# Idle matmuls, earlier casts, all score pairs ahead of the sums and a halved down-projection in batch 0 of a Linformer-attention and maxout-FFN kernel

## The chip, the cores and the metric

The kernel runs on one NeuronCore of a Trainium2 chip. The metric is the device time of one execution in microseconds (us). Span means the profiled stretch of an execution; in most of these runs it is about 1.8 to 2.1 us shorter than the time. The profile lists for every run its span and the mean granted TensorE clock, and I use the spans where a few tenths matter. All runs used here were of the state "fast". Ratios are the mean time of one kernel's fast runs over that of the other's of the same rounds, so they are not quite the ratio of the medians that I quote.

PE is TensorE, PEld its weight loads, DVE is VectorE, ACT is ScalarE, POOL is GpSimd, SP is SyncE. L203 is line 203 of that kernel's source; line numbers differ between kernels. An idle matmul is one on a zero tile whose result nobody reads. A landing is the moment when a DMA's data has arrived. "jt" counts the six slices of 128 into which the 768 hidden columns are cut. "The batch-1 projection" is the first matmul of L116, the k projection of batch 1; I use its start as the end of the tail of batch 0.

## The reference

```python
# q, k, v: (8 batches, 8 heads, 1024, 64); E, F: (64, 1024); x: (8192, 512)
k_proj = einsum('ks,bhsd->bhkd', E, k)
v_proj = einsum('ks,bhsd->bhkd', F, v)
attn   = softmax(q @ k_proj^T / 8)            # over 64 projected keys
x      = (attn @ v_proj), heads joined        # (8192, 512)
h      = max(x @ w1, x @ w2, x @ w3)          # w: (512, 768)
out    = h @ w_out                            # w_out: (768, 512)
```

## The kernel before

Eight batches run in a software pipeline: while PE does the feed-forward part of batch b, the attention of batch b+1 is woven in. Batch 0 has nothing to hide behind, so it has a hand-written head: E and F are turned, q is cast and turned, k and v are projected as their DMAs land, and the first w1 slices follow. A batch is worked in two halves of 512 tokens; half 1 of batch 0 has its sums and value products woven into the down-projection of half 0.

```python
def warmup(n, bank):                       # idle matmuls on a zero tile
    for _ in range(n):
        nc.tensor.matmul(out=ps[:, bank, :], lhsT=warm[:, 0:P], rhs=warm, start=True, stop=True)

warmup(9, 7)                               # at the very start
... cast E, F; turn them on PE; evacuate eT on VectorE, fT on ScalarE ...
q_cast0(0)                                 # even head on ScalarE, odd head on VectorE
q_cast0(1)
q_turn0(0)                                 # four 128x128 transposes, then a VectorE copy
q_cast0(2)
q_turn0(1)
k_proj0(0)                                 # 16 small matmuls, then a VectorE copy
q_cast0(3)
q_turn0(2)
k_proj0(1)
q_turn0(3)
scores0(0, 0, SB[0]); exp0(0, 0, SB[0])
for g in range(2, NPAIR):                  # NPAIR = 4
    k_proj0(g)
    scores0(0, g - 1, SB[g - 1]); exp0(0, g - 1, SB[g - 1])
    warmup(1, 3)
sums_part0(0)                              # sums of heads 0..3: PE, then 1/sum as Exp(-Ln(sum)) on ScalarE
scores0(0, 3, SB[3]); exp0(0, 3, SB[3])
warmup(1, 3)
...
v_proj0(0, 3)
sums_part0(1)
warmup(1, 2)
v_proj0(1, 3)
av0(0, 0); av0(1, 0)                       # value products, heads 0..3
norm0(0, 0, 6, (0,)); norm0(0, 1, 7, (0,)) # VectorE: product * 1/sum -> xT
v_proj0(2, 3)
warmup(1, 2)
w1_ct(0)                                   # first w1 slice, 6 matmuls
v_proj0(3, 7)
w1_ct(1, range(3))                         # second w1 slice
av0(0, 1); av0(1, 1)
norm0(0, 0, 5, (1,)); norm0(0, 1, 6, (1,))
w1_ct(1, range(3, NJT)); w1_ct(2); w1_ct(3)
...
# the feed-forward of batch 0, half 0; "slot" counts ticks, and attention pieces start at a slot
groups = [(10, q_up0), (11, scores_up0), (13, lambda: sums0(1, 4)), (15, av_up0), (19, g1[0]), ...]
# the up-projections of half 0 use up slots 1 to 12, then
for tt in range(4):
    down(0, 0, 0, tt)                      # six matmuls over jt, evacuated by ScalarE
    tick()                                 # slot 13: sums of half 1; slot 15: its value products
```

After the four `down` calls PE takes the first up-projection of half 1 (L179 in both kernels), which reads what the four normalisations of half 1 write.

The softmax here doesn't subtract the row's maximum and nothing guards it: scores larger than these inputs give would overflow.

## Time and profile before

| what | before |
|---|---|
| time, median of the first 3 runs | 401.39 us (401.13 to 401.98) |
| profiled run | 402.01 us, span 400.0 us |
| PE wait for the first q cast | 0.99 us |
| second w1 slice starts | 22.00 us |
| first down matmul to the batch-1 projection | 39.84 to 49.38 us, 9.54 us |

The page of the kernel before: the first line is busy time, share of the span and instructions of each engine; the three digit lines cut the span into 40 slices of 10 us and give busy tenths, tenths of the granted TensorE clock, and busy tenths of the DMA engines; the last is the chain of work that ended last.

```profile
PE 393.4 (98%) x2420; PEld 170.0 (43%) x2420; DVE 185.7 (46%) x268; ACT 166.3 (42%) x250; POOL 70.8 (18%) x109
...
PE   7999999999999999999999999999999999999996
...
PEclk9699999999999999999999999999999999999999
DMA  9999969999932995149970899129981111102023
...
PE 94%; DMA 2%; DVE 1%; issue 1%; ACT 1%; POOL 0%; POOLq 0%; DVEq 0%
```

PE bounds the kernel, and after 50 us nothing but PE's own matmuls does. Only the first slices hold something to gain: PE is at 7 in the first, its clock is at 6 in the second, and DMA runs at 9 through them all.

Two stretches of the windows view of the kernel before (length of the stretch; busy us of PE, PEld, DVE, ACT and POOL, each with its instructions; granted clock, DMA share, GB/s):

```profile
9.00:13.00 4.00, 3.72 (x61) 2.27 (x61) 2.24 (x9) 0.78 (x2) 1.91 (x4) 0.59 1.24 205
13.00:17.00 4.00, 4.00 (x43) 1.38 (x43) 0.23 (x1) 2.38 (x5) 1.48 (x3) 0.55 1.22 205
```

The clock stands at half for most of 9 to 17 us. The trace's clock record puts the half stretch at 9.75 to 16.58 us.

PE's part of the timeline of the kernel before (start, us, what it does, and in brackets how long PE was idle before it and what ended that):

```profile
8.24 0.70 PE L340 MATMUL ps<-ident,q_t 128*128 128x128 bf16 x8 [0.99 <-ACT q_t L345]
...
14.58 0.61 PE L296 MATMUL ps<-warm 128*128 128x512 bf16 x1
...
22.00 0.82 PE L376 MATMUL ps<-xT,w_sb 128*128 128x512 bf16 x3
...
39.84 1.46 PE L203 MATMUL ps<-wo_sb,hT 128*128 128x512 bf16 x6
41.23 0.41 PE L218 MATMUL ps<-pT,ones 64*32 64x512 bf16 x8
41.57 2.76 PE L203 MATMUL ps<-wo_sb,hT 128*128 128x512 bf16 x12
44.27 0.62 PE L218 MATMUL ps<-pT,vp 64*32 64x512 bf16 x16
...
46.75 2.70 PE L179 MATMUL ps<-xT,w_sb 128*128 128x512 bf16 x11 [0.24 <-DVE xT L257]
...
49.38 0.40 PE L116 MATMUL ps<-k_t,eT 128*64 128x512 bf16 x1
```

In the tail of batch 0, PE does six down matmuls, the sums (41.23), twelve more, the value products (44.27), the last six, and then waits a little for VectorE. ScalarE and VectorE of the same stretch:

```profile
42.88 1.06 ACT L247 ACTIVATE rinv<-lns 128x1024 f32<-128x1024 f32 x1
...
44.81 2.48 DVE L257 TENSOR_TENSOR xT<-ps,rinv 128x512 bf16<-128x512 f32 x4 [4.07 <-PE ps L218]
```

The reciprocal is ready at 43.94 us, and the four normalisations start at 44.81 on the value products (L218), not on the reciprocal.

### The profile page before, as it was taken

The page shows a single profiled execution, that of the slowest core. Times are in us where ns is not written, and L with a number is a line of the kernel's source. Part 1 is how long each engine was busy: PE and PEld are TensorE (multiplying, and loading weights), DVE is VectorE, ACT ScalarE, POOL GpSimd, SP SyncE. Part 2 cuts the span into 40 slices and gives each one's busy share as a digit, 9 for nine tenths or more (in the row PEclk, how much of TensorE's full clock was granted, in tenths as well). Part 3 has the DMA queues.
Part 4 walks back from the last instruction along what each step waited for, and adds up shares of the span by engine and source line. Part 5 has one row for each costly group of instructions (what it writes and reads, how often), then busy time and mean ns, then how long its engine had stood idle before and what let it go on. Part 6 is the DMA issues. An engine that isn't in the chain of part 4 may idle for free.

```text
span 400.0 us, 5988 instructions
## 1 busy us (share of the span) xinstructions
PE 393.4 (98%) x2420; PEld 170.0 (43%) x2420; DVE 185.7 (46%) x268; ACT 166.3 (42%) x250; POOL 70.8 (18%) x109
## 2 busy tenths in 40 slices
PE   7999999999999999999999999999999999999996
PEld 4444353444444444444444444444444444444443
DVE  3246454554744365533744256443655337433441
ACT  3413557346324553247222652245532472222222
POOL 7351141150002401060000600024010000000000
PEclk9699999999999999999999999999999999999999
DMA  9999969999932995149970899129981111102023
GB/s 220 206 209 206 207 159 197 212 163 201 163 99 66 174 181 173 62 99 172 217 151 13 159 190 231 53 66 168 201 158 60 61 52 53 54 0 107 1 104 107
DMA packets 62651, 53.73 MB, mean 134 GB/s; under 512 B 30496, under 2 KB 57632, under 8 KB 62624
## 3 DMA queue, kind: packets, MB, share of 16 engines
q0 software_dynamic: 31760, 43.52, 53.9%
q1 hardware_dynamic: 30032, 8.92, 15.7%
q10 hardware_dynamic: 832, 0.92, 0.7%
q8 instruction: 19, 0.31, 0.3%
q14 instruction: 8, 0.07, 0.0%
HBM read 57.15 MB, written 16.78 MB: 185 GB/s over the span
## 4 chain that ended last, share of the span: by engine, by line
PE 94%; DMA 2%; DVE 1%; issue 1%; ACT 1%; POOL 0%; POOLq 0%; DVEq 0%
PE ps L179 59%; PE ps L203 20%; PE ps L116 3%; PE ps L145 3%; PE ps L383 3%; PE ps L135 2%; DMA k_t<-in_k_dram 2%; PE ps L376 1%; PE ps L218 1%; DVE xT L160 1%; PE ps L238 1%; DVE xT L257 0%; PE ps L288 0%; PE ps L224 0%; PE ps L296 0%
## 5 line engine op out<-in xcount | busy, mean ns | idle before, releaser
L179 PE MATMUL ps<-xT,w_sb 128*128 128x512 bf16 x1080 | 246.6, 379 | 0.2 <-DVE xT L257 0.2
L179 PEld LDWEIGHTS <-w_sb 128*128 128x128 bf16 x1080 | 103.2, 98 | 132.7 <-issue 12.8
L184 DVE TENSOR_TENSOR m<-ps,h1s 128x512 f32<-128x512 f32 x90 | 62.2, 691 | 143.0 <-PE ps L179 114.8
L203 PE MATMUL ps<-wo_sb,hT 128*128 128x512 bf16 x378 | 91.2, 379 | 0.0
L182 ACT COPY h1s<-ps 128x512 f32<-128x512 f32 x90 | 52.7, 586 | 65.5 <-PE ps L179 65.2
L205 ACT COPY o_acc<-ps 128x512 f32<-128x512 f32 x63 | 36.9, 586 | 99.9 <-PE ps L203 99.9
L210 POOL DMA_DIRECT2D out_dram<-o_acc x30 | 21.2, 706 | 285.4 <-ACT o_acc L205 285.4
L186 DVE TENSOR_TENSOR hT<-ps,m 128x512 bf16<-128x512 f32 x90 | 62.3, 692 | 13.7 <-PE ps L179 5.2
L203 PEld LDWEIGHTS <-hT 128*128 128x128 bf16 x378 | 35.7, 98 | 47.2 <-issue 6.0
L160 DVE TENSOR_TENSOR xT<-ps,rinv 128x1024 bf16<-128x1024 f32 x28 | 32.9, 1217 | 7.8 <-PE ps L145 7.8
L138 ACT ACTIVATE pT<-ps 128x1024 bf16<-128x1024 f32 x28 | 27.1, 1021 | 13.4 <-PE ps L135 13.4
L87 POOL DMA_DIRECT2D v_t<-in_v_dram x21 | 15.3, 760 | 3.3 <-PE ps L376 1.7
L152 ACT ACTIVATE lns<-ps 128x1024 f32<-128x1024 f32 x14 | 13.6, 1021 | 1.9 <-PE ps L145 1.9
L155 ACT ACTIVATE rinv<-lns 128x1024 f32<-128x1024 f32 x14 | 14.2, 1062 | 0.0
L116 PE MATMUL ps<-k_t,eT 128*64 128x512 bf16 x56 | 13.4, 382 | 0.0
L118 PE MATMUL ps<-v_t,fT 128*64 128x512 bf16 x56 | 13.4, 382 | 0.0
L87 POOL DMA_DIRECT2D q_t<-in_q_dram x14 | 10.7, 771 | 4.3 <-DMA q_t<-in_q_dram 1.9
L383 PE MATMUL ps<-xT,w_sb 128*128 128x512 bf16 x48 | 10.9, 379 | 0.0
L87 POOL DMA_DIRECT2D k_t<-in_k_dram x14 | 10.5, 764 | 1.2 <-issue 0.6
L122 ACT CAST kp<-ps 64x512 bf16<-64x512 f32 x7 | 4.0, 578 | 15.9 <-PE ps L118 15.9
L123 DVE CAST kp<-ps 64x512 bf16<-64x512 f32 x7 | 4.8, 683 | 12.1 <-ACT kp L122 12.1
L145 PE MATMUL ps<-pT,vp 64*32 64x512 bf16 x224 | 9.1, 381 | 0.1
(79 smaller groups left out, 143.5 us busy)
## 6 DMA issues: line engine op xcount, KB each, us to landing
out_dram<-o_acc POOLq DMA_DIRECT2D x30, 512.0 KB, 3.5
q_t<-in_q_dram POOLq DMA_DIRECT2D x15, 512.0 KB, 8.4
k_t<-in_k_dram POOLq DMA_DIRECT2D x14, 512.0 KB, 13.1
v_t<-in_v_dram POOLq DMA_DIRECT2D x18, 256.0 KB, 17.7
v_t<-in_v_dram POOLq DMA_DIRECT2D x7, 512.0 KB, 16.8
w_sb<-in_moe_w_dram POOLq DMA_DIRECT2D x4, 384.0 KB, 10.3
k_t<-in_k_dram POOLq DMA_DIRECT2D x4, 256.0 KB, 8.0
w_sb<-in_moe_w_dram POOLq DMA_DIRECT2D x4, 192.0 KB, 10.1
```

The source lines that it names most:

```text
L87: nc.gpsimd.dma_start(out=dst[b % NB][:, slots], in_=sv[:, heads])
L116: nc.tensor.matmul(out=ps[0:KP, AB, :], lhsT=eT[:, si, :], rhs=k_t[i][:, :, si, :], start=(si == 0), stop=(si == SI - 1))
L138: nc.scalar.activation(out=pT[:, 2 * u + gg, :, :], in_=ps[:, AB + 2 * gg:AB + 2 * gg + 2, :], func=AF.Exp, scale=scale)
L160: nc.vector.tensor_tensor(out=xT[b % 3][:, 2 * u + half, :, :], in0=ps[:, AB + 2 * u:AB + 2 * u + 2, :], in1=rinv[u].rearrange("p (c n) -> ...
L179: nc.tensor.matmul(out=ps[:, bank, :], lhsT=w_sb[i][:, ct, jt * P:(jt + 1) * P], rhs=xT[b % 3][:, ct, ch, :], start=(ct == 0), stop=(ct == ...
L182: nc.scalar.copy(out=h1s[jt % 2], in_=ps[:, bank, :])
L184: nc.vector.tensor_tensor(out=m12[jt % 2], in0=ps[:, bank, :], in1=h1s[jt % 2], op=ALU.max)
L186: nc.vector.tensor_tensor(out=hT[c % 2][:, jt, :], in0=ps[:, bank, :], in1=m12[jt % 2], op=ALU.max)
L203: nc.tensor.matmul(out=ps[:, bank, :], lhsT=hT[c % 2][:, jt, tt * P:(tt + 1) * P], rhs=wo_sb[:, jt, :], start=(jt == 0), stop=(jt == NJT - 1))
L205: nc.scalar.copy(out=o[:, tt, :], in_=ps[:, bank, :])
L210: nc.gpsimd.dma_start(out=dst[:, tt - 1:tt + 1, :], in_=o[:, tt - 1:tt + 1, :])
L383: nc.tensor.matmul(out=ps[:, bank, :], lhsT=w_sb[i][:, ct, jt * P:(jt + 1) * P], rhs=xT[0][:, ct, 0, :], start=(ct == 0), stop=(ct == NCT ...
```

## The change

The intent is to keep PE from ever pausing long enough in batch 0 to lose its clock, to get q and the softmax sums out of the way earlier, and to let the down-projection start on three of its six jt slices before the rest is there.

```diff
+    def down_half(tt, x):                      # jt 0..2 for x = 0, jt 3..5 for x = 1
+        bank = (3 + tt) % 4
+        for jt in range(3 * x, 3 * x + 3):
+            nc.tensor.matmul(out=ps[:, bank, :], lhsT=hT[0][:, jt, tt * P:(tt + 1) * P],
+                             rhs=wo_sb[:, jt, :], start=(jt == 0), stop=(jt == NJT - 1))
+        if x: ... evacuate, and store every second tt ...
@@ ahead of the evacuation of fT
+        if y:
+            for g in (0, 1):
+                nc.scalar.copy(out=q_0[:, :, 2 * g, :], in_=q_st[:, HEAD[2 * g]])
@@ q_cast0
+        if g > 1:
             nc.scalar.copy(out=q_0[:, :, 2 * g, :], in_=q_st[:, HEAD[2 * g]])
@@ the head of batch 0
-    q_cast0(0)
-    q_cast0(1)
+    for g in range(NPAIR):
+        q_cast0(g)
+    warmup(1, 3)
     q_turn0(0)
-    q_cast0(2)
     q_turn0(1)
+    warmup(4, 3)
     k_proj0(0)
-    q_cast0(3)
     q_turn0(2)
+    warmup(1, 3)
     k_proj0(1)
-    q_turn0(3)
     scores0(0, 0, SB[0]); exp0(0, 0, SB[0])
+    q_turn0(3)
+    warmup(1, 3)
-    ... the loop over g = 2, 3 ...
     ... k_proj0(2), pair 1, warmup(2, 3), k_proj0(3), pair 2, warmup(1, 3) ...
-    sums_part0(0)
     scores0(0, 3, SB[3]); exp0(0, 3, SB[3])
-    warmup(1, 3)
+    sums_part0(0)
@@ loads and v
-    nc.gpsimd.dma_start(out=wo_sb, ...)
+    for x in range(2):
+        nc.gpsimd.dma_start(out=wo_sb[:, 3 * x:3 * x + 3], ...)
     v_proj0(0, 3)
+    warmup(1, 2)
     sums_part0(1)
+    warmup(4, 2)
+    v_proj0(1, 3)
     warmup(1, 2)
-    v_proj0(1, 3)
@@ the down-projection of half 0
-                for tt in range(4):
-                    down(0, 0, 0, tt)
-                    tick()
+                for x in range(2):
+                    for tt in range(4):
+                        down_half(tt, x)
+                        if x:
+                            tick()
```

(Cuts are marked with dots; statements are joined on a line here.)

## The prediction

> What bounds it now. The page has TensorE (PE) busy 98% of a 400.0 us span, the chain of waits is 94% PE, and from 50 us to the end the timeline shows matmuls back to back, about 216 ns apart (0.31 us at some shape changes). Only the first 50 us can be shortened; what is gained there should reach the end one for one.
>
> The head has three limits.
> (1) The clock. The clock record is full from 6.34 us, half from 9.75 to 16.58 us, full after. The Trainium skill, "TensorE: Matmul & The Clock Gate", Part 1, says that a free-running window of about 3.4 us of low PE activity halves the clock; this trace agrees: the half stretch lasts 6.83 us, two windows of 3.41 us. The window before it holds the q-cast wait (PE idle 0.99 us, to 8.24). In the half stretch a k projection takes 0.57 us instead of 0.37, a score pair 0.56 instead of about 0.31.
> (2) DMA. It is busy from 2 us to beyond 50 us, 200 GB/s or more. Landings in the trace: k groups 8.97, 10.05, 11.32, 12.61; v groups 13.91, 16.17, 17.41, 19.70; first w1 slices 18.36, 20.62.
> (3) The tail of batch 0: sums, reciprocals, four normalisations on VectorE, then the first up-projection of half 1, which waits for VectorE twice (46.75, 47.35 us).
>
> What changes. The two ACT q casts now run before the F evacuation, while ACT idles (q landed at 5.71 and 6.16), so the transposes start near 7.35 instead of 8.24 us. Eleven more idle matmuls (0.215 us warm) fill waits for k and v. I expect the clock to stay full from about 6.3 us. Then every k projection starts on its landing, sums and exps end about 2 us earlier, and PE becomes DMA-bound: last v projection 19.75 us (was 21.62), second w1 slice 20.65 us (was 22.00). From there the order is unchanged, so the gain is 1.35 us, not the roughly 3 us that half clock costs. By window phase, estimate 0.5 to 1.4.
>
> The w_out halves give some back. w_out landed at 36.40, needed at 39.84: the split load buys nothing. But nine of the down-projection's matmuls (1.94 us) move ahead of the sums. After the sums start, Ln, Exp and normalisations need 2.7 us + 2.5 us, with only nine down matmuls and the value products (2.4 us) to cover them; before, 18 matmuls covered them. Normalisation then starts limited by the reciprocal: in before's frame 45.95 instead of 44.81. Estimated loss 1.1 us, PE waiting for VectorE just before half 1.
>
> Sum: -1.35 + 1.1. Prediction 401.1 us (before 401.39), range 399.9 to 402.3; faster by over 2% 0.01, within 2% 0.98, slower by over 2% 0.01.
>
> What would show it. Right: no half-clock stretch from 6.3 us on; k_t, v_t and w_sb DMAs ending PE's waits between 9 and 21 us; second w1 slice near 20.7 us; the last wait of the first half-1 up-projection ends near 47.1 us, after PE waits on VectorE of about 1.5 us together; the batch-1 projection (49.38 us) within 0.5 us of before. Wrong: a half-clock stretch still there; or no longer wait before half 1 (then about 400 us).
>
> What would make it wrong: the DMA waits leave enough idle time for the clock to halve again; small matmuls or transposes not counting as activity; another window phase in the timed runs, which already spread 401.13 to 401.98; landings that shift.

## The result

| | before | changed |
|---|---|---|
| time, median of 6 runs | 401.38 us (400.46 to 401.98) | 401.55 us (401.41 to 402.1) |
| ratio | | 1.0006, 95% interval 0.9993 to 1.002: the same |
| second w1 slice starts | 22.00 us | 20.49 us |
| first down matmul to batch-1 projection | 9.54 us | 38.34 to 48.98 us, 10.64 us |

The page of the changed kernel, the same lines:

```profile
PE 392.9 (98%) x2432; PEld 170.0 (43%) x2432; DVE 185.8 (46%) x268; ACT 166.5 (42%) x250; POOL 71.6 (18%) x110
...
PE   8999899999999999999999999999999999999996
...
PEclk9999999999999999999999999999999999999999
DMA  8999969999922997259930899129991111102022
...
PE 92%; DMA 4%; DVE 1%; ACT 1%; issue 1%; POOL 0%; POOLq 0%; DVEq 0%
```

The dip of the clock is gone (the record is full from 5.43 us on), DMA has twice its share of the chain, and a new dip of PE stands in the fifth slice, at 40 to 50 us. PE's part of the timeline of the changed kernel:

```profile
7.45 0.61 PE L354 MATMUL ps<-ident,q_t 128*128 128x128 bf16 x8
...
13.43 0.39 PE L307 MATMUL ps<-warm 128*128 128x512 bf16 x1
...
20.49 0.82 PE L395 MATMUL ps<-xT,w_sb 128*128 128x512 bf16 x3 [0.25 <-DMA w_sb<-in_moe_w_dram]
...
38.34 3.40 PE L216 MATMUL ps<-wo_sb,hT 128*128 128x512 bf16 x15
41.67 0.41 PE L229 MATMUL ps<-pT,ones 64*32 64x512 bf16 x8
42.01 1.47 PE L216 MATMUL ps<-wo_sb,hT 128*128 128x512 bf16 x6
43.41 0.62 PE L229 MATMUL ps<-pT,vp 64*32 64x512 bf16 x16
43.97 0.82 PE L216 MATMUL ps<-wo_sb,hT 128*128 128x512 bf16 x3
45.15 0.38 PE L179 MATMUL ps<-xT,w_sb 128*128 128x512 bf16 x1 [0.36 <-DVE xT L268]
46.35 2.70 PE L179 MATMUL ps<-xT,w_sb 128*128 128x512 bf16 x11 [0.82 <-DVE xT L268]
48.98 0.40 PE L116 MATMUL ps<-k_t,eT 128*64 128x512 bf16 x1
```

In the head, the second w1 slice now starts 1.51 us earlier, and what PE waits for there is the slice's own DMA, which landed at 20.45. In the tail, fifteen down matmuls run ahead of the sums instead of six, and only nine are left to cover what follows. ScalarE and VectorE of the changed kernel in that stretch:

```profile
43.32 1.06 ACT L258 ACTIVATE rinv<-lns 128x1024 f32<-128x1024 f32 x1
...
44.41 2.48 DVE L268 TENSOR_TENSOR xT<-ps,rinv 128x512 bf16<-128x512 f32 x4 [5.18 <-ACT rinv L258]
```

Now the normalisations start on the reciprocal, which is late because the sums are. PE waits 0.36 and 0.82 us for them. The tail costs 10.64 - 9.54 = 1.10 us more, and of the 1.51 us gained in the head 0.40 is left at the batch-1 projection (49.38 against 48.98). Both spans show it: 400.0 and 399.6.

One thing did not fit the sum: the profiled run of before took 402.01 us, yet another run of the same kernel took 400.46. Before's own spread is larger than the effect under study, so the experiments had to explain it too.

### The profile page after: what moved, and what is told of

Same layout as the page of the kernel before. It is cut to its first block, busy times and chain, and to the rows that moved or that the text cites. A ratio compares the mean times of both kernels' runs of the same rounds, so it can differ in the third digit from the quotient of the medians.

```text
span 399.6 us, 6013 instructions
## 1 busy us (share of the span) xinstructions
PE 392.9 (98%) x2432; PEld 170.0 (43%) x2432; DVE 185.8 (46%) x268; ACT 166.5 (42%) x250; POOL 71.6 (18%) x110
## 4 chain that ended last, share of the span: by engine, by line
PE 92%; DMA 4%; DVE 1%; ACT 1%; issue 1%; POOL 0%; POOLq 0%; DVEq 0%
PE ps L179 59%; PE ps L203 19%; PE ps L116 3%; PE ps L145 3%; PE ps L402 3%; DMA w_sb<-in_moe_w_dram 2%; DMA k_t<-in_k_dram 2%; PE ps L135 2%; PE ps L395 1%; PE ps L216 1%; DVE xT L160 1%; DVE xT L268 0%; PE ps L299 0%; PE ps L196 0%; ACT rinv L258 0%
## 5 line engine op out<-in xcount | busy, mean ns | idle before, releaser
L203 PE MATMUL ps<-wo_sb,hT 128*128 128x512 bf16 x354 | 85.5, 379 | 0.0
L205 ACT COPY o_acc<-ps 128x512 f32<-128x512 f32 x59 | 34.6, 587 | 97.8 <-PE ps L203 97.8
L210 POOL DMA_DIRECT2D out_dram<-o_acc x28 | 20.1, 718 | 272.3 <-ACT o_acc L205 269.2
L203 PEld LDWEIGHTS <-hT 128*128 128x128 bf16 x354 | 33.6, 98 | 44.1 <-issue 5.4
L307 PE MATMUL ps<-warm 128*128 128x512 bf16 x26 | 9.4, 469 | 1.2 <-DVE ones L337 1.2
```

The lines of the kernel that those rows point to most:

```text
L203: nc.tensor.matmul(out=ps[:, bank, :], lhsT=hT[c % 2][:, jt, tt * P:(tt + 1) * P], rhs=wo_sb[:, jt, :], start=(jt == 0), stop=(jt == NJT - 1))
L205: nc.scalar.copy(out=o[:, tt, :], in_=ps[:, bank, :])
L210: nc.gpsimd.dma_start(out=dst[:, tt - 1:tt + 1, :], in_=o[:, tt - 1:tt + 1, :])
```

## The experiments

Twelve kernels ran. e1 to e4 ran on one chip, e5, e6, e7 and e9 on a second, e8 and e10 to e12 on a third, each set beside 11 runs of the kernel before. Where I compare across sets I use spans and the traces' own distances.

**Theory A**, from the prediction: the head gained by holding the clock, up to a floor set by DMA landings; the halves gave back 1.1 us by moving nine matmuls ahead of the sums. **Rivals**: B, the head is worth nothing and the halves are neutral; C, idle matmuls only occupy PE and the casts and the order do the work. Theory E came later: the gain is ScalarE doing the fourth exp ahead of Ln and reciprocal, whatever the clock.

### The runs of the kernel before, sorted by clock

The 33 runs of the kernel before beside the experiments fall into three groups by their recorded mean clock:

| recorded mean clock | runs | median us | range |
|---|---|---|---|
| 0.990 to 0.991 | 13 | 402.05 | 401.36 to 402.4 |
| 0.994 to 0.996 | 12 | 400.69 | 400.47 to 401.4 |
| 1.000 | 8 | 401.45 | 401.38 to 401.49 |

One window at half clock in a span of 400 us costs 3.41 / 400 / 2 = 0.4% of the mean clock, two cost 0.85%. So by this sum the first group lost two windows, as the profiled run did, and the second lost one. That the third group, with no loss on record, is not the fastest was a puzzle; it is taken up under e9.

### e1: the change without the w_out halves

```diff
-                for x in range(2): ... down_half(tt, x) ...
+                for tt in range(4):
+                    down(0, 0, 0, tt)
+                    tick()
```
and w_out loaded in one DMA, as before.

> The change without its w_out halves: one w_out load, the down-projection of half 0 as in the kernel before, sums after six of its matmuls. Theory A (the head gained about 1.4 us, the halves gave about 1.1 us back): about 400.45 us, 1.1 us under the changed kernel and about 1 us under the median of before; the batch-1 projection starts near 47.9 us, full clock from about 6 us on. Rival B (the head's reordering itself is worth nothing, half clock was hidden behind DMA, and the halves are neutral): 401.4 us, like both.

Measured: 400.73 us (400.62 to 400.78), ratio to before 0.998 (0.9965 to 0.9995); the batch-1 projection at 48.09 us, full clock from 5.42 us. The tail is back to 9.54 us (38.55 to 48.09). B is out. The time is 0.3 us above what was expected; the second w1 slice landed at 20.66 here and was used at 20.71, against 20.45 and 20.49 in the profiled run of the changed kernel, which is most of that.

### e2: before, with the halves alone

```diff
-                for tt in range(4): down(0, 0, 0, tt); tick()
+                for x in range(2):
+                    for tt in range(4):
+                        down_half(tt, x)
+                        if x: tick()
```
and w_out loaded in two DMAs.

> The kernel before with the w_out halves alone. Theory A: about 1.1 us slower than before, near 402.5 us, with PE waiting for VectorE about 1.2 us in two stretches just before half 1, and the normalisation starting on the reciprocal. Rival B: 401.4 us, as before.

Measured: 401.93 us (401.35 to 402.37), ratio 1.0013 (0.9996 to 1.0029). By the median only half of the expected loss shows, and the interval holds 1. The trace shows it whole: first down matmul at 38.26, batch-1 projection at 48.90, 10.64 us, with the same two waits of 0.36 and 0.82 us on VectorE. The profiled run had lost one clock window only (7.90 to 11.31 us), so its second w1 slice started at 20.42, about as early as in the changed kernel. The six runs drew other clock states than the 11 runs beside them; a median over states is a poor measure of 1 us here. Sorted by recorded clock, the four runs at 0.994 to 0.996 have a median span of 399.85 us, against 398.7 for the three of before in the same set: 1.15 us more. The two runs at 0.991 have 400.6 against 400.1, only 0.5 us more; neither was profiled, and why they lose less stays open.

### e3: the halves kept, the sums early again

```diff
-                        if x:
+                        if (x, tt) in ((0, 1), (1, 0), (1, 1), (1, 3)):
                             tick()
```

> The changed kernel, halves kept, but the sums emitted after six of the down matmuls and the value products after eighteen, as in before. If the loss is the order (nine matmuls moved ahead of the sums), this recovers all of it: about 400.45 us, like the head-only run. If the loss comes from the halves themselves (four banks held open, a second w_out load), it stays at 401.5 us.

Measured: 400.4 us (400.24 to 400.67), ratio 0.9973 (0.9958 to 0.9989). Spans are 398.5 to 398.9, e1's 398.6 to 398.8. PE's timeline of this run:

```profile
38.44 1.46 PE L216 MATMUL ps<-wo_sb,hT 128*128 128x512 bf16 x6
39.83 0.41 PE L229 MATMUL ps<-pT,ones 64*32 64x512 bf16 x8
40.17 2.76 PE L216 MATMUL ps<-wo_sb,hT 128*128 128x512 bf16 x12
42.87 0.63 PE L229 MATMUL ps<-pT,vp 64*32 64x512 bf16 x16
...
45.35 2.70 PE L179 MATMUL ps<-xT,w_sb 128*128 128x512 bf16 x11 [0.24 <-DVE xT L268]
47.98 0.40 PE L116 MATMUL ps<-k_t,eT 128*64 128x512 bf16 x1
```

Six matmuls, sums, twelve, value products: the distance is 9.54 us again, with the halves and the two loads still there. So the loss is the order, and nothing else about the halves costs anything that shows. This run moved the sums by nine matmuls and the value products by three; that the sums are what counted is read from the changed kernel's trace, where the value products end at 44.03 us, the reciprocal at 44.38, and the normalisations start at 44.41. Nor do they gain anything: the second part of w_out landed at 36.27 us in the changed kernel, before the first down matmul at 38.34.

### e4: e1 without the added idle matmuls

```diff
-    warmup(1, 3)      # ahead of q_turn0(0), ahead of k_proj0(1), ahead of k_proj0(2)
-    warmup(4, 3)      # ahead of k_proj0(0)
-    warmup(2, 3)      # ahead of k_proj0(3); one is kept
-    warmup(1, 2) ... warmup(4, 2) ... warmup(1, 2)   # around sums_part0(1), v_proj0(1); one is kept
```

> The head-only version without the eleven added idle matmuls (three kept, as before), casts and order kept. Theory A (idle matmuls keep the clock up): the clock record shows a half-clock stretch of 3.4 or 6.8 us again in most runs, and the time is 0.5 to 1 us above the head-only run, near 401.2 us. Rival C (the casts and the order did it, idle matmuls only occupy PE): full clock, and 400.4 us or a little less.

(The count in this text is off: the change adds twelve, and this kernel has 13 idle matmuls, one fewer than before.)

Measured: 400.55 us (400.28 to 400.74), ratio 0.9976 (0.9961 to 0.9991). The profiled run was at half clock from 8.35 to 15.17 us, two windows, and lost nothing:

```profile
13.96 0.63 PE L249 MATMUL ps<-qT,kpT 64*64 64x512 bf16 x2
...
20.72 0.82 PE L391 MATMUL ps<-xT,w_sb 128*128 128x512 bf16 x3
...
48.10 0.40 PE L116 MATMUL ps<-k_t,eT 128*64 128x512 bf16 x1
```

A score pair takes 0.63 us, as in the half stretch of before, but the second w1 slice (landed 20.68) and the batch-1 projection stand where e1 has them, 20.71 and 48.09. My expectation failed: losing the clock cost nothing here. With q cast early and the exps in a row, PE at half speed still reached the landings in time. That spoke for C and led to theory E.

### e9: before, with the fourth score pair ahead of the sums

```diff
-    sums_part0(0)
     scores0(0, 3, SB[3])
     exp0(0, 3, SB[3])
+    sums_part0(0)
     warmup(1, 3)
```

> The kernel before with one swap: the fourth k score pair and its exp ahead of the first half of the sums. Theory E (the gain of the head comes from ACT doing the fourth exp before the Ln and the reciprocal, whatever the clock): 400.6 to 400.8 us, little spread, though some runs have half clock. Rival A (the idle matmuls or the casts did it): the three groups of before stay, median 401.4 us.

Measured: 400.66 us median, but 400.58 to 401.97, ratio 0.9982 (0.9963 to 1.0): four runs at 400.58 to 400.67, two at 401.93 and 401.97. Theory E falls; the swap alone does not protect every run. Three of the four quick runs have a recorded clock of 0.995 or 0.996, a group in which before itself takes 400.69 us, so the better median is mostly a matter of the states drawn. The profiled run was one of the slow ones, and it solves the puzzle of the clock column. The windows view of this run says full clock for 13.00 to 16.90 us:

```profile
13.00:16.90 3.90, 3.90 (x29) 1.18 (x27) 0.28 (x2) 1.92 (x4) 1.06 (x2) 1.00 1.22 206
```

Its timeline says otherwise, by an idle matmul in that stretch and one after it:

```profile
14.96 0.61 PE L296 MATMUL ps<-warm 128*128 128x512 bf16 x1
...
17.78 0.39 PE L296 MATMUL ps<-warm 128*128 128x512 bf16 x1
...
21.88 0.82 PE L376 MATMUL ps<-xT,w_sb 128*128 128x512 bf16 x3
```

The first entry of this run's clock record is at 16.95 us. What lies before the first entry is counted as full, but the same matmul took 0.61 us there and 0.39 after. PE had run at half clock from the start to 16.95 us. A recorded mean of 1.00 can therefore mean "never lost" or "never had until late". The group of before at 401.45 us with a clock of 1.000 probably is of the second kind; no profile of before fell into it, so that stays open.

### e6: before, with the early casts alone

```diff
+        if y:
+            for g in (0, 1):
+                nc.scalar.copy(out=q_0[:, :, 2 * g, :], in_=q_st[:, HEAD[2 * g]])
```
and these two casts taken out of `q_cast0`.

> The kernel before with only the two q casts moved ahead of the F evacuation. Theory D (the casts matter little, because the first k group lands at 8.97 us anyway): as before, 401.4 us, with the same three groups by clock (400.7, 401.4, 402.1). Rival (the late transposes are what delays the head): about 400.6 us with little spread.

Measured: 401.9 us (401.25 to 402.03), ratio 1.0004 (0.9989 to 1.0019). Its profiled run happened to meet the same clock windows as before's (half from 9.75 to 16.57 us), which makes the two traces a pair: the second w1 slice starts at 21.88 instead of 22.00, the batch-1 projection at 49.26 instead of 49.38. The early casts alone are worth about 0.1 us in that state. Five of the six runs are of the two-window group (0.990 to 0.991) and took 401.69 to 402.03 us, so theory D holds: the casts alone do not make the head fast. The transposes do start at 7.43 us, and then PE waits 0.80 us for k, which landed at 8.80.

### e10: both, the casts and the swap

> The kernel before with the early q casts and the fourth score pair ahead of the sums, no added idle matmul. If these two together are what made the no-idle version fast in every clock state: 400.3 to 400.8 us in all runs. If that version owed it to its few idle matmuls or to a lucky window phase: runs with two half-clock windows near 401.9 us, as with either part alone.

Its edit is the sum of e9's and e6's. Measured: 400.78 us (400.73 to 401.16), ratio 0.9995 (0.9982 to 1.0008). The three runs with two half windows took 401.08, 400.78 and 401.16 us: better than either part alone, not quite all of it. The profiled run was at half clock from 8.42 to 15.25 us, nearly e4's windows. Its second w1 slice starts at 21.06, 0.45 us after the landing at 20.61; e4's started 0.04 us after. What e4 has beyond this is the further reordering of casts and transposes and one idle matmul fewer.

### e8: before in its own order, with five more idle matmuls

```diff
     q_cast0(0)
     q_cast0(1)
+    warmup(4, 3)
     q_turn0(0)
     ...
     q_turn0(2)
+    warmup(1, 3)
     k_proj0(1)
```

> The kernel before, its order untouched, with five idle matmuls more: four in the wait for the first q cast, one in the wait for the second k group. If holding the clock is what the head's gain needs (theory A), the runs show full clock from about 6 us and 400.6 to 400.9 us with little spread, median 0.7 us under before. If the order of ACT's work is what matters (theory E), the time stays at 401.4 us or more whatever the clock.

Measured: 400.67 us (400.59 to 400.76, all five runs with a clock of 0.999 to 1.0), ratio 0.9989 (0.9977 to 1.0002); before had many fast draws this time, with a median of 400.75, so the interval holds 1 and the times alone do not show a gain; what they show is that no run was slow, where 5 of before's 11 took 401.4 us or more. The profiled run:

```profile
7.19 1.04 PE L296 MATMUL ps<-warm 128*128 128x512 bf16 x4
...
20.59 0.82 PE L378 MATMUL ps<-xT,w_sb 128*128 128x512 bf16 x3 [0.28 <-DMA w_sb<-in_moe_w_dram]
```

The record is full from 6.00 us and the second slice starts on its landing. The whole gain of e1's head is here with nothing reordered: five idle matmuls, four of them in one hole. The hole of 0.99 us is filled, and the clock that before loses at 9.75 us is kept. So theory A holds for before's order when it would lose two windows, and e4 shows that the new order does not need it.

### e11: e4 without the nine idle matmuls at the start

```diff
-    warmup(9, 7)
```

> A stress test: the no-idle version without the nine idle matmuls at the start either, so that the clock stays low until the head's own work raises it. If the clock no longer matters once the order is changed (theory E): 400.4 to 400.9 us. If the no-idle version only had slack for a half-clock stretch that ends by about 15 us (theory A in a weaker form, the clock matters once PE's work falls behind the landings): low clock until about 16 us, second w1 slice past 21.5 us, 401.2 to 401.9 us.

Measured: 401.43 us, 400.61 to 402.49, ratio 1.001 (0.9993 to 1.0028). The overhead outside the span varied in this set of runs, so the spans are clearer: four runs at 398.6 to 398.8 us, like e4, and two at 400.3 and 400.5. The profiled run, of span 398.7, got its clock at 14.37 us and lost nothing. The new order has slack for half clock up to about 15 us, as two traces show (14.37 here, 15.17 in e4). That the two slow runs got their clock later is likely, but they were not profiled.

### e7: the floor, by taking DMA away (wrong result)

```diff
-    for g in range(NPAIR - 1):
-        load0(v, v_t, g)
+    load0(v, v_t, 0)                 # groups 1..3 are not loaded; all use group 0's data
-            load0(v, v_t, NPAIR - 1)
-                                 rhs=v_t[0][:, HEAD[2 * g + u], si, :], ...
+                                 rhs=v_t[0][:, u, si, :], ...
-    warmup(4, 2)                     # around v_proj0(1), built on e1
-    warmup(1, 2)
```

> Wrong result on purpose: the head-only version without the loads of v groups 1 to 3 of batch 0 (all groups use group 0) and without the five idle matmuls that covered the wait for group 1. If the head is bound by DMA landings, the second w1 slice is used at 19.0 to 19.4 us instead of 20.7 and the time falls 1.2 to 1.5 us below the head-only run, to about 399.3 us. If PE's chain bounds it, the slice is used at 20.5 us and the time stays at 400.7 us.

Measured: 398.95 us (398.75 to 399.37), ratio 0.9934 (0.992 to 0.9949); the result is wrong, as meant. The second w1 slice starts at 19.22 us:

```profile
19.22 0.82 PE L392 MATMUL ps<-xT,w_sb 128*128 128x512 bf16 x3
```

The median span is 1.5 us under e1's (397.2 against 398.7), as expected; the times, from two chips, differ by 1.78. With the landings earlier (the slice landed at 16.53) the head moves. The five idle matmuls that are gone as well are not the reason: e4 has none of them, and its slice still started at 20.72, with the landing at 20.68. So DMA landings are what stops the head at about 20.5 us. That is why full clock gains 1.5 us and not the 3 us or so that half clock takes from PE.

### e5: value products of half 1 earlier

```diff
-                      (13, lambda: sums0(1, 4)), (15, av_up0),
+                      (13, lambda: sums0(1, 4)), (14, av_up0),      # built on e1
```

> The head-only version with batch 0's value products for half 1 emitted six down matmuls earlier. In before's frame the normalisation could start at 43.98 (reciprocal ready) instead of 44.81, which covers the two PE waits of 0.24 and 0.17 us beyond the matmul pace and the 0.4 us of the other: if the tail of batch 0 is bound by this VectorE chain, about 0.57 us faster than the head-only run, near 400.15 us, and the batch-1 projection 9.0 us after the first down matmul instead of 9.54. If the tail is bound by PE's own work, no change.

Measured: 400.38 us (400.1 to 401.16), ratio 0.9971 (0.9956 to 0.9987).

```profile
39.86 0.41 PE L229 MATMUL ps<-pT,ones 64*32 64x512 bf16 x8
...
41.60 0.63 PE L229 MATMUL ps<-pT,vp 64*32 64x512 bf16 x16
42.16 2.76 PE L203 MATMUL ps<-wo_sb,hT 128*128 128x512 bf16 x12
44.76 2.75 PE L179 MATMUL ps<-xT,w_sb 128*128 128x512 bf16 x12
47.44 0.40 PE L116 MATMUL ps<-k_t,eT 128*64 128x512 bf16 x1
```

The waits on VectorE are gone, and from the first down matmul at 38.47 it is 8.97 us to the batch-1 projection, 0.57 less than e1, as expected. The six runs spread: their spans are 398.1 to 399.2 us with a median of 398.35, 0.35 under e1's 398.7, and the longer ones were not profiled. This is the change's down-projection idea turned round: more of PE's work behind the sums and the value products, not ahead of them.

### e12: e5, with the second pair of value products of half 0 ahead of the second w1 slice

```diff
     v_proj0(3, 7)
-    w1_ct(1, range(3))
     av0(0, 1)
     av0(1, 1)
     ...
-    w1_ct(1, range(3, NJT))
+    w1_ct(1)
```

> Candidate: the version with early value products, and in half 0 the second pair of value products ahead of the second w1 slice, so that the wait for that slice's landing overlaps the normalisation. Expected 0.15 us under the early-value run in the same state, near 400.1 us; if the wait for the slice is not what sets the pace there, no change.

Measured: 399.87 us (399.73 to 400.88), ratio 0.9969 (0.9954 to 0.9983). Four runs have spans of 397.7 to 397.9, against e5's best of 398.1: 0.2 to 0.4 us better, more than expected. The profiled run was the slow one of the five, with half clock up to the first entry of the record at 10.29 us:

```profile
8.46 1.91 PE L307 MATMUL ps<-warm 128*128 128x512 bf16 x4
10.30 0.44 PE L235 MATMUL ps<-eT,k_t 128*64 128x64 bf16 x16
```

Here the idle matmuls themselves seem to do harm: at half clock, four of them take 1.91 us instead of the 1.03 of e1, and k, which landed at 8.89, waits until 10.30. No run without them in this state tests it. Up to the second w1 slice this is the head of the changed kernel, so its clock is not always there in time either: this run's span is 398.9 us, the four others' 397.7 to 397.9. This version is the fastest of all the correct ones; why its fast runs beat the expectation was not traced.

## Why the prediction was right or wrong

- **The time**: 401.1 us was predicted, 401.55 measured, inside the range of 399.9 to 402.3, and the same within noise. Right, but this tests little: the range covers the whole spread of before (400.46 to 401.98), so a change worth nothing would have fallen inside it too. The sum also takes 1.35 us, read in a run of 402.01 us that lost two windows, from a median of 401.39 over mixed states. Within the profiled pair it does better: the sum says 0.25 us less, and the spans fell by 0.4 (400.0 to 399.6).
- **The head's gain**: 1.35 us expected from the second w1 slice (22.00 to 20.65); the slice moved to 20.49, 1.51 us. The last v projection was put at 19.75 and came at 19.81. Right, and bound by landings as said: e7 moves it by moving DMA.
- **The halves**: a loss of 1.1 us from nine matmuls ahead of the sums. The trace shows 1.10 us, e2's trace shows the same in before, and e3 takes it away by moving the sums and the value products back. The start of the normalisations was put at 45.95 in before's frame, as set by the reciprocal; it came at 44.41, which is 45.91 in that frame (the first down matmul came 1.50 us earlier). The last wait was put near 47.1 us and ended at 46.94. Right. "The split load buys nothing" is right by e3.
- **The clock**: the record is full from 5.43 us, as foreseen. The Trainium skill, "TensorE: Matmul & The Clock Gate", Part 1, says that the windows are free-running and of about 3.4 us; 3.41 and 6.83 us stretches at different places in the traces here agree.
- **Wrong in part: what the clock gives.** The step "By window phase, estimate 0.5 to 1.4" was too high at its low end. Before's 12 runs that lost one window have a median of 400.69 us, and e1's is 400.73: against those runs the head gains nothing. The profiled run of e2, which has before's head and lost one window, shows why: its second w1 slice started at 20.42 us, 0.05 after its landing, so nothing was left to gain. The change removes most of the slow states (402.05 and 401.45) of before, not time from its good one. Twelve idle matmuls were not needed for that: five in before's order do it (e8), and e4 did without any added ones in all its five runs.
- **Wrong count**: the prediction says eleven added idle matmuls; there are twelve. Nothing rests on it.

So the changed kernel is before with its head freed, nearly, of the clock lottery, and with a tail that its order makes 1.1 us longer (seen in both traced runs with it). The two cancel in the median. One of its six runs took 402.1 us; it was not profiled, so it stays unexplained. e12's slow run, with the same head and a clock that came only at 10.29 us, shows one way in which that can happen.

## What to carry to other kernels

When a reduction feeds another engine's chain (here Ln, reciprocal, four normalisations, some 5 us), put independent matmuls after it, not ahead of it: in the traces here, the same nine matmuls ahead of the sums cost 1.10 us more than behind them, and moving six more behind the value products gained 0.57 us. Before filling a clock dip, ask what waits behind it: here DMA landings capped the gain at 1.5 us, and an order with slack made the dip free as long as it ended by about 15 us. And sort the runs by clock state, reading matmul durations and not the record alone, before believing a difference of a few tenths of a per cent.

## What the Trainium skill lacked or had wrong

- The table in "TensorE: Matmul & The Clock Gate", Part 1, gives an idle window as what halves the clock. In the kernel before, the window that ended at 9.75 us was not idle: from 6.40 to 9.70 us PE was busy for 2.24 of 3.30 us, and the clock was halved all the same; in e4 a window with PE busy for 2.85 us (4.93 to 8.35) ended in half clock too. A later passage of the same part does tell of a kernel whose clock swings because of short idles between groups of matmuls. How much activity a window needs is not stated in either.
- The same part says that about 3.4 us of sustained activity raise the clock. In e9 PE was busy nearly without a break from 1.19 us to beyond 7 us (nine 128x512 matmuls, then 32 of 128x64), and the clock came only at 16.95 us; in e12, after a start of the same kind, at 10.29 us. The phase of the windows is not all of it. Counted back from these times in steps of 3.41 us (my estimate of where the windows lie), a window from 3.30 to 6.71 us in e9 and one from 3.46 to 6.87 in e12 had PE busy throughout and did not raise the clock. That small matmuls count for less does not explain it either: in e2 the window from 7.90 to 11.31 us held k projections, transposes and the start of one score pair, busy for 3.34 us, and raised it. What is counted stays open.
- The same part warns that the clock events of a trace can be unreliable. It does not say that in the profile's clock column the time before the first event reads as full clock: 1.00 in e9 from 13.00 to 16.90 us, while an idle matmul took 0.61 us against 0.39 later.
- It calls the cost of the ramp (the slow start) under 1% of a typical span. What the clock states cost here, lost windows included, is of that order: about 1.4 us of 401 between the groups at 402.05 and 400.69. But that is far more than the change's net effect in the medians (0.17 us). The page says that the number of slow matmuls varies with the phase of the windows; it does not say that the times of one kernel fall into groups, here 0.6 and 0.8 us apart.
